# Two gated long convolutions: phases of two units on four row tiles, cosines in SBUF, one N=96 spectrum shape, and a new order

## The chip, the cores and the metric

The kernel runs on one core of one Trainium2 chip. The metric is the device time of one execution in microseconds. The engines are TensorE (PE, whose weight loads are listed apart as PEld), VectorE (DVE), ScalarE (ACT), GpSimd (POOL) and SyncE (SP, which here only issues DMAs). DVE, ACT and PE reach PSUM; POOL works on SBUF alone.

## The reference

Two diagonal state-space layers A and B read the same input `u` (2048 positions, 512 channels). Each has 128 complex modes a channel. A gate mixes the two outputs:

```python
A = -jnp.exp(log_A_real) + 1j * A_imag
C = (C_real + 1j * C_imag) * dt[:, None]
P = jnp.exp((A * dt[:, None])[:, :, None] * pos[None, None, :])
K = 2.0 * jnp.einsum("dn,dnl->dl", C, P).real          # a kernel of 2048 taps for each channel
y = jnp.fft.irfft(jnp.fft.rfft(K, L2) * jnp.fft.rfft(u_t, L2), L2)[:, :, :L]
...                                                    # y + u * D_skip is a (or b)
g = _sigmoid((x * gate_w).sum(-1, keepdims=True))
return g * a + (1 - g) * b
```

## The kernel before

**Units.** Layer and channel together give 1024 rows; 16 of them make a unit, so there are 64 units. For a unit the kernel writes the tap index as l = 64 m + q (32 values of m, 64 of q) and each mode's term as a product of one factor in m and one in q. Each factor is a decay times a cosine or sine:

- `phase` computes turns for the q half (`p0s`) and the m half (`p1s`) on PE, eight f16 matmuls in four accumulation steps: constants `cph` against `ones` or against `rot`, which holds the modes' turns. The q half uses rows 0 to 63 of the array, the m half rows 64 to 127, so the two are two row tiles. `rot` is read back from a bounce in DRAM by `turns`.
- `magnitude`, `cosine`, `sine` on ACT: |turns|, then two Sin. The copy for the cosine (`p0c`, `p1c`) lies in PSUM, as `p0s` and `p1s` do.
- `grid0` and `grid1` on POOL (L520) build the decay factors `f0` (16 x 64 for each partition) and `f1` (16 x 32) from the table `bas` of 28 shifts for each row, filled by `make_bases` on ACT (L488). The table's layout is row by shift, so each of ACT's writes of one shift has a step of 28 elements and POOL's reads of eight shifts are contiguous.
- `cos_minus`, `cos_plus`, `sin_minus`, `sin_plus`, `one_cos`, `one_sin` on DVE (L543 to L563) multiply decay by cosine or sine: one input in SBUF, one in PSUM. The cosine products are written to the free half of `f0` and `f1`, the sine products over the decay.
- `modes` on PE (L571) contracts over the modes into `pk`, one bank for each unit; `keep` (ACT, L578) copies it to `ks`, `skip` (DVE, L581) adds the skip term to tap 0.

**Blocks.** Four units are a block; there are 16. Transforms are matmuls in two steps: `first` (L593), `s2` (L630). `xall` holds the half-transformed data: kernels of an even block, 32 columns of products `t2`, kernels of an odd block, and inputs `u` of two blocks. For an even block `s2` multiplies 32 kernels (N=64, in two column tiles of 64 weights each), for an odd block 32 kernels and the inputs of the next two blocks (N=128, full weights). `products` (DVE, L641) multiplies the kernel spectrum in PSUM with the input spectrum `v`, once for the real part's rows and once turned. For that `keep_v` (ACT, L650) copies two blocks' input spectra out of PSUM, `turn_v` and `both_v` (SP DMAs) move halves between partitions, and `negate_v` (DVE, L661) writes the negated half from SBUF to SBUF. `add_products` (POOL DMAs with add) joins the two products, `inverse` (PE, L679) and `keep_z` (ACT, L685) go back, and `final` with its copies and DMAs turns four finished blocks at a time into output. `gate` (L760), once at the start, sums `u * gate_w` over channels for all positions, with the result on all 128 partitions.

**Order.** Every operation is recorded in a list and then built in the order of the table `ORDER` (2462 numbers); each engine executes its instructions in just that order. `SLOTS` names the PSUM bank of each PSUM tile. The grids' buffers `f0` and `f1` are two deep, so POOL's grid for a unit waits for `modes` of the unit two before.

```python
    for n in ORDER or range(len(ops)):
        key, name, fn, args = ops[n]
        fn(*args)
```

Of the kernel before, what the change touches and what calls it, by code (L numbers as in the profile page):

```python
# [11 lines left out]
F32 = mybir.dt.float32  # L12
# [174 lines left out]
]  # L187


SLOTS = [  # L190
    int(c) for c in (
        "012121212013230145460125463737251467615702561324560702376267021420713301314031031731206743"
# [804 lines left out]
```

## Time and profile before

| | |
|---|---|
| timed runs, us | 568.38, 570.80, 572.99 (median 570.8) |
| span of the profiled execution, us | 568.5 (nothing that lies around it is listed) |
| mean granted TensorE clock | 0.921 |
| PE, PEld, DVE, ACT, POOL busy, us | 458.2, 371.7, 412.8, 426.0, 342.6 |
| instructions | 26964 |
| costliest group on each engine | POOL L520 203.4 us, PE L630 109.4, DVE L641 91.4, ACT L488 50.6 |
| DMA | 49.84 MB, 88 GB/s on average |

A row of the view of groups reads: line, engine, operation, output <- inputs, shapes, count | busy us together, mean ns of one | idle time of the engine before them and what ended it. Busy time is the union of the instructions' spans: instructions of ACT and DVE overlap their neighbours by 0.05 to 0.2 us, and matmul rows include their latency, so that start to start times are shorter than the means. A matmul on f32 data shows as two rows of the trace. A row of the waits reads: engine and line that waited <- who ended the wait: us in total, times, longest.

### The profile page before, as it was taken

Reading aid. Unit: us, or ns where it says so; the run is one execution under the profiler, and the core shown is the slowest. Engines: PE = TensorE matmul, PEld = TensorE weight load, DVE = VectorE, ACT = ScalarE, POOL = GpSimd, SP = SyncE. Lnnn points to the kernel's source line nnn. Section 1 sums busy time; section 2 is a strip of 40 time slices with the busy share of each in tenths; the row PEclk is TensorE's granted clock in tenths of the full one; section 3 lists DMA queues with packets and bytes.
Section 4 is the critical chain, followed back from the end, with each engine's and each line's share of the span. In section 5 each row is a group of like instructions: output and inputs, shape, how many; then the busy total and the mean of one; then the engine's idle time right before and its main releaser. Section 6 shows DMA issues by size and latency. Waiting matters only on the chain.

```text
span 568.5 us, 26964 instructions
## 1 busy us (share of the span) xinstructions
PE 458.2 (81%) x11888; PEld 371.7 (65%) x11888; DVE 412.8 (73%) x826; ACT 426.0 (75%) x967; POOL 342.6 (60%) x324
## 2 busy tenths in 40 slices
PE   8557986879777898868997986968997979859756
PEld 8445456657575676767775774856785757748746
DVE  7096876888967983798689855698689896788210
ACT  4788879969986998867997994949987777565311
POOL 1549986989999877346766653435727664455120
PEclk9797989989988997998999996989997997989779
DMA  3649423460423515044506323044505250163242
GB/s 102 216 130 315 188 58 50 105 131 22 91 48 89 110 38 114 33 98 83 110 7 134 81 51 76 32 96 91 95 21 115 40 96 22 31 131 64 44 74 77
DMA packets 30772, 49.84 MB, mean 88 GB/s; under 512 B 10048, under 2 KB 15680, under 8 KB 30656
## 3 DMA queue, kind: packets, MB, share of 16 engines
q1 hardware_dynamic: 25536, 31.34, 18.6%
q0 software_dynamic: 5120, 16.78, 17.8%
q8 instruction: 93, 1.52, 1.1%
q14 instruction: 23, 0.19, 0.1%
HBM read 17.18 MB, written 5.77 MB: 40 GB/s over the span
## 4 chain that ended last, share of the span: by engine, by line
PE 29%; ACT 17%; DVE 15%; issue 7%; POOL 5%; DMA 1%; ACTq 0%; DVEq 0%; POOLq 0%
PE pk L571 6%; PE psi L679 6%; DVE xall L641 5%; PE p0s L504 5%; DVE v L661 4%; ACT bas L488 4%; PE ps L630 4%; PE ps L593 3%; PE pf L699 3%; ACT xall L600 2%; PE pl L733 1%; ACT p1c L510 1%; ACT z L685 1%; ACT p0c L516 1%; ACT p0c L510 1%
## 5 line engine op out<-in xcount | busy, mean ns | idle before, releaser
L520 POOL TENSOR_TENSOR f<-bas 128x512 f32<-128x512 f32 (+1 forms) x128 | 203.4, 1670 | 119.1 <-PE pk L571 49.3
L630 PE MATMUL ps<-xall,gk 128*64 128x64 f32 (+1 forms) x1728 | 109.4, 252 | 13.3 <-ACT v L650 4.3
L630 PEld LDWEIGHTS ps<-xall,gk 128*64 128x64 f32 (+1 forms) x1728 | 102.4, 155 | 24.8 <-issue 6.6
L641 DVE TENSOR_TENSOR xall<-ps,v 128x256 f32<-128x256 f32 x256 | 91.4, 418 | 26.1 <-PE ps L630 21.1
L571 PE MATMUL pk<-f,f 128*32 128x64 f32 x4096 | 79.1, 231 | 23.7 <-DVE f L551 13.2
L571 PEld LDWEIGHTS pk<-f,f 128*32 128x32 f32 x4096 | 67.3, 117 | 35.0 <-issue 24.4
L669 POOL DMA_DIRECT2D xall<-xall x64 | 60.0, 1203 | 48.0 <-ACT z L685 22.6
L679 PE MATMUL psi<-mi,xall 128*128 128x128 f32 x512 | 74.8, 303 | 11.4 <-DMA xall<-xall 6.8
L679 PEld LDWEIGHTS psi<-mi,xall 128*128 128x128 f32 x512 | 67.8, 211 | 22.5 <-issue 10.7
L559 DVE TENSOR_TENSOR f<-f,p1c 128x512 f32<-128x512 f32 x64 | 43.7, 684 | 25.8 <-ACT p1c L516 23.8
L543 DVE TENSOR_TENSOR f<-f,p0c 128x512 f32<-128x512 f32 x64 | 43.6, 683 | 24.5 <-ACT p0c L516 22.6
L504 PE MATMUL p0s<-cph,ones 64*128 64x512 f16 x128 | 52.8, 412 | 9.2 <-ACT xall L600 3.9
L593 PE MATMUL ps<-w,ks 64*64 64x64 f32 x2048 | 41.9, 231 | 16.2 <-issue 8.1
L685 ACT COPY z<-psi 128x512 f32<-128x512 f32 x64 | 38.5, 620 | 21.5 <-PE psi L679 21.5
L504 PE MATMUL p1s<-cph,ones 64*128 64x512 f16 x128 | 53.0, 414 | 0.7 <-DVE f L559 0.7
L593 PEld LDWEIGHTS ps<-w,ks 64*64 64x64 f32 x2048 | 36.6, 144 | 25.3 <-issue 11.8
L504 PE MATMUL p0s<-cph,rot 64*128 64x512 f16 x128 | 52.4, 409 | 0.2 <-issue 0.2
L504 PE MATMUL p1s<-cph,rot 64*128 64x512 f16 x128 | 52.4, 409 | 0.0
L488 ACT ACTIVATE bas<-dec 128x128 f32<-128x128 f32 x192 | 50.6, 490 | 0.8 <-DVE dec L423 0.7
L510 ACT ACTIVATE p1c<-p1s 128x512 f32<-128x512 f32 x64 | 38.2, 597 | 16.9 <-PE p1s L504 8.1
L510 ACT ACTIVATE p0c<-p0s 128x512 f32<-128x512 f32 x64 | 38.8, 607 | 15.4 <-PE p1s L504 5.7
L563 DVE TENSOR_TENSOR f<-f,p1s 128x512 f32<-128x512 f32 x64 | 43.7, 684 | 5.7 <-ACT p1s L513 4.3
(130 smaller groups left out, 866.7 us busy)
## 6 DMA issues: line engine op xcount, KB each, us to landing
xall<-xall POOLq DMA_DIRECT2D x64, 256.0 KB, 5.3
v<-v SPq DMA_DIRECT2D x64, 128.0 KB, 3.3
uraw<-in_us SPq DMA_DIRECT2D x16, 256.0 KB, 4.2
z<-in_ut SPq DMA_DIRECT2D x16, 256.0 KB, 6.8
out_dram<-ot SPq DMA_DIRECT2D x24, 128.0 KB, 2.4
par<-in_par SPq DMA_DIRECT2D x8, 256.0 KB, 5.2
gk<-in_gk SPq DMA_DIRECT2D x4, 512.0 KB, 7.0
eg<-in_eg SPq DMA_DIRECT2D x4, 512.0 KB, 7.2
```

What stands on the lines that cost most here:

```text
L488: S.activation(bas[:, c % 2, :, j], decays[c][:, 0], AF.Exp, scale=-float(s))
L504: PE.matmul(ps, w[h : h + 64], cph[h : h + 64, j], start=j == 0, stop=j == 3, tile_position=(h, 0))
L510: S.activation(pc[u], ps[u], AF.Abs)
L520: G.tensor_tensor(o.rearrange("p k (a b) -> p k a b", b=8), x[:, :, hi : hi + n].unsqueeze(3).to_broadcast([128, 16, n, 8]), x[:, :, lo : ...
L559: V.tensor_tensor(f[:, 0], f[:, 1], p1c[u], OP.mult)
L571: PE.matmul(pk[32 * kd : 32 * kd + 32, i, :], f1[:, p, 4 * i + kd, :], f0[:, p, 4 * i + kd, :], start=p == 1, stop=p == 0, tile_position=( ...
L593: PE.matmul(ps[h][64 * ri : 64 * ri + 64, n, :], x[r], w1[r, ri, r], start=True, stop=True, tile_position=(64 * h, 64 * ri),)
L630: PE.matmul(ps[h : h + w, j, 0:n], gk[:, k, h : h + w], xall[:, x0:x1, 2 * k : 2 * k + 2], start=True, stop=True, tile_position=(0, h),)
L641: V.tensor_tensor(k.rearrange("p x (k t) -> p k x t", t=2), p2s[b, g][:, :, 0:64].rearrange("p k (x t) -> p k x t", t=2), vv.unsqueeze(3). ...
L669: G.dma_start(out=xk(b)[o, s], in_=t2[t, s], accum_op=OP.add)
L679: PE.matmul(ps[:, i, :], xk(b)[:, x : x + 2, :].rearrange("p x k -> p (x k)"), mi, start=True, stop=True)
L685: S.copy(z[:, :, d0 : d0 + 4], pis[b, g].rearrange("p i r -> p r i"))
```

## The change

- **Phases.** `phase` handles two units at once on four row tiles of 32 rows: the q halves of both on tiles 0 and 1 (N=512), the m halves on tiles 2 and 3, whose steps with `rot` are two matmuls of N=256 each. `rot` is laid out for that and loaded by six DMAs a chunk of eight units instead of two.
- **Cosines in SBUF.** `p0c` and `p1c` become SBUF tiles (four buffers), so the three cosine products read two SBUF inputs. The sine products come first and go to the free half; the cosine products go over the decay. `pk` and `ks` hold two units, so `keep` and `skip` run 32 times, not 64.
- **Spectra.** `xall` holds 32 kernels, the inputs of one odd block, of one even block, 32 kernels, then `t2`. Blocks 0 to 14 all use N=96 with full weights; the last block N=64; the input of block 0 alone N=32. `keep_v` runs for every block (128 copies of 128 elements instead of 64 of 256).
- **Second products.** `negate_v` goes. A DMA `same_v` copies the half, and the product takes the sign from `halfs`, +1 or -1 for each partition: two scalar-tensor-tensors with a step of 2 instead of one tensor-tensor. `v` is now turned for each block: 96 DMAs instead of 64.
- **Decay table.** `bas` is shift by row: ACT writes contiguously, POOL reads the shifts with a step of 128 elements.
- **Gate.** `gate_parts` sums four channel groups into 32 partitions each (four column tiles), `gate_keep` copies to SBUF, and a matmul with 1/32 everywhere sums them.
- **Order.** `ORDER` and `SLOTS` are new.

```diff
-    11, 2, 0, 6, 1, 3, 4, 5, 74, 15, 19, 20, 21, 23, 22, 25, 24, 29, 40, 26, 27, 45, 12, 28, 18,
+    11, 0, 1, 19, 20, 21, 22, 23, 24, 5, 74, 25, 26, 28, 27, 30, 31, 32, 75, 33, 29, 34, 4, 2, 35, 36, 40, 37, 45,
...
-    t2 = xall[:, 32:64]
+    t2 = xall[:, 96:128]
-    rot = const.tile([128, 2, 8, 128], F16, name="rot")
-    bas = const.tile([128, 2, 128, 28], F32, name="bas")
+    rot = const.tile([128, 2, 4, 2, 128], F16, name="rot")
+    bas = const.tile([128, 2, 28, 128], F32, name="bas")
...
-    def phase(u):
-        p0s[u], p1s[u] = bank("p0s"), bank("p1s")
+    def phase(q):
+        us = (2 * q, 2 * q + 1)
+        ps = [bank(n) for n in ("p0s", "p0s", "p1s", "p1s")]
+        for n, u in enumerate(us):
+            p0s[u], p1s[u] = ps[n], ps[2 + n]
+        w = rot[:, q // 4 % 2, q % 4]
         for j in range(4):
-            for h, ps in ((0, p0s[u]), (64, p1s[u])):
-                w = rot[:, u // 8 % 2, u % 8] if j % 2 else ones
-                PE.matmul(
-                    ps, w[h : h + 64], cph[h : h + 64, j], start=j == 0, stop=j == 3, tile_position=(h, 0)
-                )
+            for h in range(2):
+                for t in range(4):
+                    rows = slice(32 * t, 32 * t + 32)
+                    halves = j % 2 and t > 1
+                    if h and not halves:
+                        continue
+                    cols = slice(256 * h, 256 * h + 256) if halves else slice(0, 512)
+                    PE.matmul(
+                        ps[t][:, cols], w[rows, h] if j % 2 else ones[rows], cph[rows, j, cols],
+                        start=j == 0, stop=j == 3 and h == (t > 1), tile_position=(32 * t, 0),
+                    )
 
     def magnitude(u, ps, pc, name):
-        pc[u] = bank(name)
+        pc[u] = work.tile([128, 512], F32, name=name, tag="pc", bufs=4)
...
     def grid(u, o, hi, n, lo):
-        x = bas[:, u // 8 % 2, 16 * (u % 8) : 16 * (u % 8) + 16, :]
+        x = bas[:, u // 8 % 2, :, 16 * (u % 8) : 16 * (u % 8) + 16].rearrange("p s k -> p k s")
...
     def s2(b, g):
-        x0, x1 = 64 * (b % 2), 64 * (b % 2) + 32
+        x0, x1 = 48 * (b % 2), 48 * (b % 2) + 48
         if b < 0:
-            x0 = x1
-        if b % 2 and b < nblk - 1:
-            x1 += 32
+            x1 = x0 + 16
+        elif b == nblk - 1:
+            x0 += 16
...
     def products(b, g, second):
...
+        if second:
+            for t in range(2):
+                V.scalar_tensor_tensor(o[:, :, :, t], k[:, :, :, t], halfs, vv, op0=OP.mult, op1=OP.mult)
+        else:
+            V.tensor_tensor(o, k, vv.unsqueeze(3).to_broadcast([128, 4, 32, 2]), OP.mult)
...
-    def negate_v(i, h):
-        V.tensor_scalar(v_at(hi, i, 1, h), v_at(hi, i, 0, h), -1.0, None, op0=OP.mult)
+    def same_v(b, h):
+        dma(v_at(hi, b, 1, h), v_at(hi, b, 0, h))
...
+    def gate_parts(j):
+        psg[j] = bank("psg")
+        for sb in range(nsb):
+            PE.matmul(
+                psg[j][32 * sb : 32 * sb + 32], gw[:, sb : sb + 1].to_broadcast([128, 32]), ut(sb, j),
+                start=True, stop=True, tile_position=(0, 32 * sb),
+            )
```

**On PE, a unit's phases.** The first steps of the first unit stood so before (`p0s_357` and `p1s_358` are its two banks):

```order
L504 LDWEIGHTS ones_73
L504 MATMUL p0s_357<-cph_72,ones_73 128x512
L504 LDWEIGHTS ones_73
L504 MATMUL p1s_358<-cph_72,ones_73 128x512
L504 LDWEIGHTS rot_83
L504 MATMUL p0s_357<-cph_72,rot_83 128x512
L504 LDWEIGHTS rot_83
L504 MATMUL p1s_358<-cph_72,rot_83 128x512
```

The step with `rot` of the first pair now, with one bank for each row tile (`p0s_402` and `p1s_404` belong to the pair's first unit):

```order
L493 LDWEIGHTS rot_84
L493 MATMUL p0s_402<-cph_72,rot_84 128x512
L493 LDWEIGHTS rot_84
L493 MATMUL p0s_403<-cph_72,rot_84 128x512
L493 LDWEIGHTS rot_84
L493 MATMUL p1s_404<-cph_72,rot_84 128x256
L493 LDWEIGHTS rot_84
L493 MATMUL p1s_405<-cph_72,rot_84 128x256
L493 LDWEIGHTS rot_84
L493 MATMUL p1s_404<-cph_72,rot_84 128x256
L493 LDWEIGHTS rot_84
L493 MATMUL p1s_405<-cph_72,rot_84 128x256
```

Four banks are filled in the steps that filled two, and a step with `rot` has six matmuls for two units where it had four.

**On DVE, around the products of a block.** Before, near the end of an odd block, the negations of the next input spectra (L661) stand between products (L641) and the cosine and sine products of later units:

```order
L641 TENSOR_TENSOR xall_78<-ps2_2645,v_77 128x4x32x2 x2
L547 TENSOR_TENSOR f0_2545<-f0_2545,p0c_2557 128x16x32
L551 TENSOR_TENSOR f0_2545<-f0_2545,p0s_2492 128x16x32
L555 SCALAR_TENSOR_TENSOR f0_2545<-f0_2545,p0s_2492 128x16x32
L581 TENSOR_TENSOR ks_2705<-pk_2655,dl_75 128x4
L661 TENSOR_SCALAR v_77<-v_77 64x512
L641 TENSOR_TENSOR xall_78<-ps2_2711,v_77 128x4x32x2 x2
L559 TENSOR_TENSOR f1_2707<-f1_2707,p1c_2717 128x512
L661 TENSOR_SCALAR v_77<-v_77 64x512
```

Now, in a block's products (L644 the first, L642 the second of a group):

```order
L547 TENSOR_TENSOR f0_2401<-f0_2401,p0c_2431 128x16x32
L644 TENSOR_TENSOR xall_79<-ps2_2489,v_78 128x4x32x2
L543 TENSOR_TENSOR f0_2401<-f0_2401,p0c_2431 128x16x32
L644 TENSOR_TENSOR xall_79<-ps2_2506,v_78 128x4x32x2
L551 TENSOR_TENSOR f1_2527<-f1_2527,p1s_2409 128x512
L555 TENSOR_TENSOR f1_2350<-f1_2350,p1c_2438 128x512
L642 SCALAR_TENSOR_TENSOR xall_79<-ps2_2506,small_69,v_78 128x4x32 x2
L642 SCALAR_TENSOR_TENSOR xall_79<-ps2_2476,small_69,v_78 128x4x32 x2
L642 SCALAR_TENSOR_TENSOR xall_79<-ps2_2496,small_69,v_78 128x4x32 x2
```

No negation is left, a second product is a pair of instructions, and among them stand cosine products (L543, L547, L555) whose two inputs, `f0` or `f1` and `p0c` or `p1c`, are both in SBUF.

More of the change, by code (lines that the diff above doesn't have):

```diff
@@ L278, in fixed @@
         V.memset(ones, ONE_W)
-        V.memset(rot[32:64], 0.0)
+        G.memset(thirty, 1.0 / 32)
         for b in range(2):
-            G.memset(bas[:, b, :, 0:24].rearrange("p c (s b) -> p c s b", b=8)[:, :, :, 0], 1.0)
+            G.memset(bas[:, b, 0:24].rearrange("p (s b) c -> p s b c", b=8)[:, :, 0], 1.0)
     def warm_up(n):
@@ L480, in turns @@
         i = next(i for i, cs in enumerate(BATCHES) if c in cs)
-        for h, t in zip((0, 64), dsps[i]):
-            src = t[BATCHES[i].index(c)].rearrange("(u k) d n -> (k d) u n", u=8)
-            dma(rot[h : h + 32 * (1 + h // 64), c % 2], src)
+        two, four = (t[BATCHES[i].index(c)] for t in dsps[i])
+        two = two.rearrange("(q u k) d n -> u (k d) q n", q=4, u=2)
+        four = four.rearrange("(q u s k) d n -> u s (k d) q n", q=4, u=2, s=2)
+        for u in range(2):
+            dma(rot[32 * u : 32 * u + 32, c % 2, :, 0], two[u])
+            for h in range(2):
+                dma(rot[64 + 32 * u : 96 + 32 * u, c % 2, :, h], four[u, h])
     def make_bases(c, n):
@@ L571, in modes, with keep, skip @@
                     PE.matmul(
-                        pk[32 * kd : 32 * kd + 32, i, :], f1[:, p, 4 * i + kd, :], f0[:, p, 4 * i + kd, :],
-                        start=p == 1, stop=p == 0, tile_position=(0, 32 * kd),
-                    )
-    def keep(u):
-        kss[u] = work.tile([128, 4, Q], F32, name="ks", tag="ks", bufs=4)
-        S.copy(kss[u], pks[u])
-    def skip(u):
-        V.tensor_tensor(kss[u][:, :, 0], pks[u][:, :, 0], dl[:, 4 * u : 4 * u + 4], OP.add)
+                        pks[q][32 * kd : 32 * kd + 32, 4 * h + i, :], f1[:, p, 4 * i + kd, :],
+                        f0[:, p, 4 * i + kd, :], start=p == 1, stop=p == 0, tile_position=(0, 32 * kd),
+                    )
+    def keep(q):
+        kss[q] = work.tile([128, 8, Q], F32, name="ks", tag="ks", bufs=2)
+        S.copy(kss[q], pks[q])
+    def skip(q):
+        V.tensor_tensor(kss[q][:, :, 0], pks[q][:, :, 0], dl[:, 8 * q : 8 * q + 8], OP.add)
     def xk(b):
@@ L602, in first_k @@
     def first_k(q):
-        first(q, "ps1", [kss[u][:, i, :] for u in (2 * q, 2 * q + 1) for i in range(4)])
+        first(q, "ps1", [kss[q][:, i, :] for i in range(8)])
     def keep_x(q, h):
@@ L760, in gate, with gate_keep @@
             PE.matmul(
-                psg[j], gw[:, sb : sb + 1].to_broadcast([128, 128]), ut(sb, j), start=sb == 0, stop=sb == nsb - 1
-            )
+                psg[j][32 * sb : 32 * sb + 32], gw[:, sb : sb + 1].to_broadcast([128, 32]), ut(sb, j),
+                start=True, stop=True, tile_position=(0, 32 * sb),
+            )
+    def gate_keep(j):
+        S.copy(ut(0, j), psg[j])
+    def gate(j):
+        psg[j] = bank("psg")
+        PE.matmul(psg[j], thirty, ut(0, j), start=True, stop=True)
     def gate_sig(j):
@@ L793, in unit @@
     def unit(u):
+        if u % 2 == 0:
+            op("ph", phase, u // 2)
         for name, fn in (
-            ("ph", phase), ("g0", grid0), ("g1", grid1),
-            ("a0", lambda u: magnitude(u, p0s, p0c, "p0c")), ("c0", lambda u: cosine(u, p0c)),
-            ("s0", lambda u: sine(u, p0s)), ("a1", lambda u: magnitude(u, p1s, p1c, "p1c")),
-            ("c1", lambda u: cosine(u, p1c)), ("s1", lambda u: sine(u, p1s)),
-            ("cm", cos_minus), ("cp", cos_plus), ("sm", sin_minus), ("sp", sin_plus), ("oc", one_cos),
-            ("os", one_sin), ("mo", modes), ("ke", keep), ("kd", skip),
+            ("g0", grid0), ("g1", grid1),
+            ("a0", lambda u: magnitude(u, p0s, p0c, "p0c")), ("s0", lambda u: sine(u, p0s)),
+            ("a1", lambda u: magnitude(u, p1s, p1c, "p1c")), ("s1", lambda u: sine(u, p1s)),
+            ("c0", lambda u: cosine(u, p0c)), ("c1", lambda u: cosine(u, p1c)),
+            ("sm", sin_minus), ("sp", sin_plus), ("os", one_sin), ("cm", cos_minus), ("cp", cos_plus),
+            ("oc", one_cos), ("mo", modes),
         ):
@@ L803, in unit @@
         if u % 2:
-            op("f1", first_k, u // 2)
+            q = u // 2
+            op("ke", keep, q)
+            op("kd", skip, q)
+            op("f1", first_k, q)
             for h in range(2):
-                op("xk", keep_x, u // 2, h)
+                op("xk", keep_x, q, h)
     def inputs(b):
@@ L814, in block @@
     def block(b):
-        nxt = b % 2 and b < nblk - 1
         for g in range(8):
@@ L826, in block @@
                     op("ya", add_products, b, h, x)
-        if nxt:
+        if b < nblk - 1:
             for h in range(2):
-                for i in range(2):
-                    op("vt", turn_v, i, h)
-                    op("vn", negate_v, i, h)
-                    op("vb", both_v, i, h)
+                op("vt", turn_v, b + 1, h)
+                op("vs", same_v, b + 1, h)
+                op("vb", both_v, b + 1, h)
     def back(b):
@@ L842, in tile_gated_s4d @@
     inputs(0)
-    inputs(1)
     chunk(0)
@@ L864, in tile_gated_s4d @@
         b, n = divmod(u, 4)
-        if b % 2 and n < 2 and b < nblk - 1:
-            inputs(b + 1 + n)
+        if n == 1 and b < nblk - 1:
+            inputs(b + 1)
         if n == 3:
@@ L887, in tile_gated_s4d @@
     last = {}
-    for n in ORDER or range(len(ops)):
+    for n in ORDER:
         key, name, fn, args = ops[n]
@@ L948, in _layout, with spread @@
     eg = np.tile(np.repeat(eg, 2, 0), (2, 1, 1, 1))
-    e16 = np.eye(16)
-    x = np.kron(e16, np.arange(32) + 0.5)
-    w = np.kron(e16, m - 16.0)
-    o = np.kron(e16, np.ones(32))
-    cph = np.zeros((2, 64, 4, 512))
-    cph[0, :32, 1] = np.stack([x, x / LOW], 1).reshape(32, 512)
-    cph[1, :, 1] = np.stack([w, w / LOW, o, o / LOW], 1).reshape(64, 512)
+    def spread(rows, d):
+        return np.einsum("ef,dj->edfj", np.eye(rows), np.stack(d)).reshape(rows * len(d), -1)
+    cph = np.zeros((4, 32, 4, 512))
+    x, w, o = np.arange(32) + 0.5, m - 16.0, np.ones(32)
+    cph[0:2, :, 1] = spread(16, [x, x / LOW])
+    cph[2:4, :, 1] = np.tile(spread(8, [w, w / LOW, o, o / LOW]), 2)
     cph[:, 0, 0], cph[:, 0, 2] = ONE_M, -ONE_M
@@ L958, in _layout @@
     cph = cph.reshape(128, 4, 512)
-    kern = np.arange(128) % 2
-    small = np.concatenate([ldt, 1 - 2 * kern[:, None], gw], 1)
+    kern = np.arange(128)[:, None] % 2
+    half = np.arange(128)[:, None] // 64
+    small = np.concatenate([ldt, 1 - 2 * kern, 1 - 2 * half, gw], 1)
     arrs = dict(
```

111 lines of the change are left out of this document (53 added, 58 removed), and 288 rows, old and new, of tables (ORDER, SLOTS).

## The prediction

> **What bounds the kernel now.** I read the busy times of the page first, then the middle of the run by windows, then the waits.
>
> ```profile
> PE 458.2 (81%) x11888; PEld 371.7 (65%) x11888; DVE 412.8 (73%) x826; ACT 426.0 (75%) x967; POOL 342.6 (60%) x324
> ...
> 30.00:540.00 510.00, 420.13 (x11249) 336.01 (x11250) 396.95 (x765) 402.62 (x915) 329.36 (x306) 0.93 0.37 84
> ...
> 100.00:150.00 50.00, 40.94 (x993) 33.01 (x995) 43.90 (x87) 45.14 (x102) 46.09 (x48) 0.97 0.37 83
> 150.00:200.00 50.00, 39.32 (x924) 31.26 (x916) 39.95 (x76) 41.57 (x98) 45.55 (x47) 0.93 0.41 84
> ```
>
> Columns of a window row: its length, then busy us of PE, weight loads, DVE, ACT and POOL (instructions in brackets), then the granted TensorE clock. Three engines are at 78 to 82% from 30 to 540 us, so no single one is the bound. The waits say the same:
>
> ```profile
> POOL f L520 <- PE pk L571: 49.3, 16, 6.0
> ...
> DVE f L559 <- ACT p1c L516: 23.8, 22, 3.0
> DVE f L543 <- ACT p0c L516: 22.6, 15, 12.3
> ...
> ACT z L685 <- PE psi L679: 21.5, 17, 8.3
> DVE xall L641 <- PE ps L630: 21.1, 15, 8.3
> ```
>
> POOL waits for PE (a grid buffer comes free when `modes` has read it), DVE for ACT's cosines and for PE, ACT for PE: a ring in which each hands on to the next.
>
> ```profile
> PE 29%; ACT 17%; DVE 15%; issue 7%; POOL 5%; DMA 1%; ACTq 0%; DVEq 0%; POOLq 0%
> ```
>
> The chain that ended last is spread over the same three. My estimate is therefore a sum over PE, DVE and ACT, and the middle 510 us is scaled by it; the first 30 and last 28.5 us I leave alone. The profiled execution's span is 568.5 us; what lies around it isn't listed, and the timed runs' median, 570.8, stands 2.3 us above it, which I add at the end.
>
> **The change part by part.**
>
> *Four row tiles* (L504 before). A unit's phases are four steps, two matmuls each:
>
> ```profile
> 300.14 0.39 PE L504 MATMUL p0s<-cph,ones 64*128 64x512 f16 x1
> 300.15 0.39 PE L504 MATMUL p1s<-cph,ones 64*128 64x512 f16 x1
> 300.37 0.38 PE L504 MATMUL p0s<-cph,rot 64*128 64x512 f16 x1
> 300.37 0.38 PE L504 MATMUL p1s<-cph,rot 64*128 64x512 f16 x1
> ...
> L504 PEld LDWEIGHTS <-ones 64*128 64x128 f16 x256 | 14.4, 98 | 25.3 <-issue 12.4 <-DVE f L547 1.2 <-DVE f L543 0.2
> ```
>
> The two of a step start 0.01 us apart, and steps start 0.22 us apart: the row tiles run together. A unit costs 4 x 0.22 = 0.88 us, 64 units 56 us. If four tiles run together as two do, a pair of units takes the same four steps (the second tile pair's 256-column halves follow each other inside a step), 32 x 0.88 = 28 us: **PE -28**. If they don't, 0; I take -28, the nearer row. A pair's 20 weight loads replace 16; I price them at nothing, since loads here run under the previous step's 0.22 us, and without that cover a load is 0.10 us. The Trainium skill's "TensorE: Matmul & The Clock Gate", Part 3, measured speedups, gives 3.07x, not 4x, for four row tiles at N=512; by that the step would stretch to 0.29 us and the gain would be about 19 us, an estimate. The trace of before shows two tiles at full overlap and never four.
>
> *N=96 spectra* (L630).
>
> ```profile
> L630 PE MATMUL ps<-xall,gk 128*128 128x128 f32 x448 | 55.3, 279 | 7.3 <-ACT v L650 4.3 <-ACT xall L600 2.9
> L630 PE MATMUL ps<-xall,gk 128*64 128x64 f32 x1280 | 54.1, 242 | 6.1 <-DVE xall L641 2.3 <-issue 1.4 <-DVE f L559 1.2
> L760 PE MATMUL psg<-z,small 128*128 128x512 f32 x32 | 14.8, 605 | 0.0
> ```
>
> A row costs 0.123 us at N=128 with all 128 columns of weights, and 0.042 us at N=64 with half of them. Fifteen blocks now have 64 rows each at N=96 and full weights, between 2 x 0.042 = 0.084 us and 0.123: 81 to 118 us. The last block keeps 128 x 0.042 = 5.4, the first has 128 rows at N=32, at most 5.4. Against 109.4 that is -18 to +20. Halfway by columns, 0.104, gives 100 + 11: **+1**.
>
> *Tiled gate* (L760): 32 rows at 0.46 us become four groups of 4 column tiles, two rows deep, and 8 rows of the summing matmul: 16 x 0.46 = 7.4. **PE -7**. If the column tiles ran one after the other it would be +4.
>
> *DVE.*
>
> ```profile
> L641 DVE TENSOR_TENSOR xall<-ps,v 128x256 f32<-128x256 f32 x256 | 91.4, 418 | 26.1 <-PE ps L630 21.1 <-issue 3.6 <-DMA rot<-dsp 0.4
> L661 DVE TENSOR_SCALAR v<-v 64x512 f32<-64x512 f32 x32 | 41.1, 1298 | 0.8
> L581 DVE TENSOR_TENSOR ks<-pk,dl 128x4 f32<-128x4 f32 x64 | 10.3, 161 | 35.3 <-ACT ks L578 34.9
> ...
> 12.05 0.28 DVE L383 TENSOR_TENSOR tb<-tb,sg 128x128 f32<-128x128 f32 x1
> 12.26 0.28 DVE L390 SCALAR_TENSOR_TENSOR rc<-rc,g 128x128 f32<-128x128 f32 x1
> ```
>
> The negations go: **-41**. Half of the 64 skip adds go: **-5**. Each of 128 second products (91.4/256 = 0.357 us) becomes two scalar-tensor-tensors of 128 elements. Such a one starts 0.21 us after its neighbour and lasts 0.28: 256 of them cost 54 to 72 instead of 46. I take the start to start, since they stand in pairs: **+8**. The cosines, read from SBUF, I price at 0.68 us as now, without a wait (the third rival is that wait).
>
> *ACT.*
>
> ```profile
> L488 ACT ACTIVATE bas<-dec 128x128 f32<-128x128 f32 x192 | 50.6, 490 | 0.8 <-DVE dec L423 0.7
> L685 ACT COPY z<-psi 128x512 f32<-128x512 f32 x64 | 38.5, 620 | 21.5 <-PE psi L679 21.5
> ...
> L578 ACT COPY ks<-pk 128x256 f32<-128x256 f32 x64 | 25.6, 402 | 28.2 <-PE pk L571 28.1
> L650 ACT COPY v<-ps 128x256 f32<-128x256 f32 x64 | 23.7, 397 | 12.1 <-DVE xall L641 8.7 <-PE ps L630 2.2 <-issue 0.6
> ...
> 265.27 0.35 ACT L357 ACTIVATE axy<-par 128x128 f32<-128x128 f32 x1
> 265.49 0.30 ACT L358 ACTIVATE pa<-par 128x128 f32<-128x128 f32 x1
> ```
>
> The 192 decay exponentials write every 28th element and take 50.6/192 = 0.264 us each; 128-element instructions with contiguous output stand 0.22 us apart. Turned, they save 0 to 8: **-8**. Kernel copies: 64 of 0.40 become 32 of 0.60, **-6**. Spectrum copies: 64 of 0.37 become 128 of 0.22 to 0.30, **+4 to +15**, I take **+8**. Gate copies: 4 x 0.60, **+2**. Abs into SBUF instead of PSUM: 0 (the SBUF copy's 0.60 is what Abs takes now).
>
> *Queues.*
>
> ```profile
> v<-v SPq DMA_DIRECT2D x64, 128.0 KB, 3.3
> ```
>
> SP issues 32 more copies of `v` and three times as many loads of `rot`. A block's chain from `keep_v` to products is paid every block instead of every second one, but it runs a block ahead, under four units' work; uncovered, it would be two landings in a row, 2 x 3.3 = 6.6 us a block.
>
> *Sum.* PE 458 - 28 + 1 - 7 = 424; DVE 413 - 41 - 5 + 8 = 375; ACT 426 - 8 - 6 + 8 + 2 = 422. Together 1221 against 1297, -5.9%. The middle becomes 510 x 0.941 = 480; with 58.5 around it 538.5, and **541 us** with the 2.3. ACT would stand at 78% of the span, below the 90% it holds from 100 to 150 us (45.14 of 50), so the sum asks nothing that this kernel doesn't reach already.
>
> **The rivals.**
>
> *Grids read at a stride.*
>
> ```profile
> L520 POOL TENSOR_TENSOR f<-bas 128x1024 f32<-128x1024 f32 x64 | 136.2, 2129 | 10.4 <-ACT bas L488 6.5 <-PE pk L571 3.9
> L520 POOL TENSOR_TENSOR f<-bas 128x512 f32<-128x512 f32 x64 | 76.9, 1211 | 108.7 <-PE pk L571 45.3 <-issue 23.4 <-DVE f L543 16.9
> ```
>
> The turned table makes POOL read its eight shifts 128 elements apart. No row shows POOL reading so. From 100 to 200 us POOL is 92% busy, 43 us of it grids (14 + 14 by the two rows' means: 28 of some 1.6 us), so there a grid that lasts half longer adds about 21 us to the path, and little elsewhere: 538 + 21 + 2 = **562 us**. The Trainium skill's "GPSIMD Engine Reference", Performance pitfalls for Q7 kernels, says that reads with a step above 8 bytes cost half more per element; no run here shows it yet.
>
> *DVE and POOL shut each other out.* Why the negations are so dear:
>
> ```profile
> 249.41 0.42 DVE L661 TENSOR_SCALAR v<-v 64x512 f32<-64x512 f32 x1
> ...
> 250.66 4.79 DVE L661 TENSOR_SCALAR v<-v 64x512 f32<-64x512 f32 x2
> ...
> 250.66 1.36 POOL L520 TENSOR_TENSOR f<-bas 128x512 f32<-128x512 f32 x1
> ...
> 252.26 2.55 POOL L520 TENSOR_TENSOR f<-bas 128x1024 f32<-128x1024 f32 x1
> ```
>
> Alone such an instruction takes 0.42 us; with grids running two took 4.79, and the mean is 1.30: 0.88 us of waiting each. It works from SBUF to SBUF. After the change 192 products (two `cos`, one `one_cos` a unit) have both inputs in SBUF. If each waits as the negation did, DVE gets 192 x 0.88 = 169 us more: 375 + 169 = 544. DVE's best window is 88% (43.90 of 50), so the span would be 544 / 0.88 = 618. At half that wait, 460 us busy, DVE needs 522 and decides nothing; it is slower than before from about 125 us of waits, 0.65 us each. Some waits would overlap idle time, so I price this case at **600 us**. Against it: a negation writes as well as reads at double rate, the products do not, and they need not meet POOL in the same way. The Trainium skill's "SBUF — State Buffer", Who interferes with whom, names just these, a DVE instruction with two SBUF inputs against a GpSimd instruction that reads SBUF, as exclusive; the trace agrees for the negation (0.42 to 4.79 us for two) and has no such product beside a grid.
>
> *The tiles don't run together, or the ring turns no faster.* Without the 28 us of PE, and with each wait that goes replaced by the next in the ring, 566 to 576: **570**.
>
> **How the numbers follow.** A measurement of this kernel can tell about 1% from no change: 565 to 576.5 is the same. The forecast, 525 to 555, gets 0.53; faster still, where the engines overlap better than now (ACT 422 at 82% of 515), 0.10; the strided grids 0.13, two thirds of it still faster; the unchanged ring 0.06; DVE and POOL shut out 0.18. Faster is 0.53 + 0.10 + 0.09 = 0.72, same 0.04 + 0.06 = 0.10, slower 0.18. By the open prices alone the sum's low end is 1221 - 19 (N=96) - 4 (spectrum copies) = 1198, 532 us; its high end 1221 + 28 (row tiles) + 19 (N=96) + 11 (gate) + 18 (second products) + 8 (decay) + 7 (spectrum copies) = 1312, 577 us. The range is 515 to 595: it takes these in, and leaves out a tenth above and less below.
>
> **What would show it.** Right: phase steps of four matmuls 0.22 us apart; N=96 rows about 0.10 us; DVE busy near 375 us with `cos` products at 0.68; ACT's decay at 0.22; spectrum products no longer waiting for copies of `v`. Wrong: products of `cos` at 1 us and more with the spread of the negations, grids at 2.9 and 1.6 us, DVE above 460 us busy, or POOL above 400.

## The result: 647.4 us against 570.5, and the profile after

The changed kernel takes 647.4 us (median of four runs, 644.9 to 649.5), the kernel before 570.5 in the runs beside it: a ratio of 1.135, 95% interval 1.129 to 1.140. The forecast was 541 us. The profiled execution's span is 646.2 us at a granted clock of 0.865 (before 568.5 at 0.921). Here and below a time is the median of all runs of a kernel, while a ratio and its 95% interval leave out runs that stand apart from the others, slow ones mostly, so the two can differ a little.

The page's busy times of the changed kernel, then two windows from its middle (length, then busy us of PE, weight loads, DVE, ACT, POOL, then the granted clock):

```profile
PE 483.9 (75%) x11512; PEld 420.5 (65%) x11512; DVE 514.5 (80%) x889; ACT 424.9 (66%) x1003; POOL 452.3 (70%) x325
...
200.00:300.00 100.00, 77.24 (x2196) 65.70 (x2196) 85.09 (x131) 75.11 (x174) 83.88 (x60) 0.90 0.34 74
300.00:400.00 100.00, 76.90 (x1856) 68.52 (x1859) 86.13 (x147) 68.54 (x175) 72.58 (x56) 0.85 0.36 76
```

ACT is where the forecast had it (424.9 against 422). DVE, forecast at 375, has 514.5, and POOL 452 in place of 343. In the middle DVE is now the busiest engine, at 85 to 86%, while PE and ACT, 82% and 79% busy in the middle before, have fallen back to 77% and 69 to 75%. The groups of DVE and POOL (count, then busy us and mean ns of one, then the idle time before them and what ended it) say what grew:

```profile
L555 DVE TENSOR_TENSOR f<-f,p1c 128x512 f32<-128x512 f32 x64 | 92.1, 1443 | 5.0 <-ACT p1c L506 3.8
L642 DVE SCALAR_TENSOR_TENSOR xall<-ps,small,v 128x128 f32<-128x128 f32 x256 | 84.1, 425 | 41.5 <-ACT v L648 25.3 <-PE ps L624 13.1 <-DMA xall<-xall 2.5
L547 DVE TENSOR_TENSOR f<-f,p0c 128x512 f32<-128x512 f32 x64 | 80.5, 1260 | 1.3 <-ACT p0c L506 0.9
L543 DVE TENSOR_TENSOR f<-f,p0c 128x512 f32<-128x512 f32 x64 | 79.6, 1244 | 0.6
L644 DVE TENSOR_TENSOR xall<-ps,v 128x256 f32<-128x256 f32 x128 | 50.9, 414 | 16.3 <-PE ps L624 8.9 <-ACT v L648 6.2 <-ACT bas L722 1.0
L551 DVE TENSOR_TENSOR f<-f,p1s 128x512 f32<-128x512 f32 x64 | 43.4, 677 | 7.3 <-POOL f L510 5.5 <-ACT p1s L503 1.5
...
L510 POOL TENSOR_TENSOR f<-bas 128x1024 f32<-128x1024 f32 x64 | 188.7, 2952 | 41.7 <-PE pk L565 25.2 <-DVE f L547 5.4 <-DVE f L551 2.7
L510 POOL TENSOR_TENSOR f<-bas 128x512 f32<-128x512 f32 x64 | 111.6, 1746 | 47.2 <-PE pk L565 46.7 <-issue 0.3
```

A sine product (L551, its second input in PSUM) still takes 0.68 us. The three cosine products, of the same shape with both inputs in SBUF, take 1.24 to 1.44: (1443 + 1260 + 1244 - 3 x 680) ns x 64 = 122 us more than before. The grids take 2.95 and 1.75 us in place of 2.13 and 1.21. Two stretches of the timeline (start, us, engine) show the two engines together:

```profile
470.56 0.67 DVE L533 TENSOR_TENSOR f<-f,p0s 128x512 f32<-128x512 f32 x1
471.16 5.91 DVE L547 TENSOR_TENSOR f<-f,p0c 128x512 f32<-128x512 f32 x1
...
470.13 1.78 POOL L667 DMA_DIRECT2D xall<-xall  x1
470.71 3.97 POOL L510 TENSOR_TENSOR f<-bas 128x1024 f32<-128x1024 f32 x1
473.42 1.68 POOL L359 TENSOR_TENSOR rc<-rc,g 128x128 f32<-128x128 f32 x1
473.83 2.68 POOL L510 TENSOR_TENSOR f<-bas 128x512 f32<-128x512 f32 x1
```

The sine product of 470.56 takes 0.67 us. The cosine product behind it starts 0.45 us after a grid and ends at 477.07, 0.56 us after the second grid (476.51): it sat out both grids and the small product between them. The grids are stretched as well, but less than the 3.97 us of the first one suggests: that row begins while POOL's DMA issue of 470.13 still runs (to 471.91), which leaves 2.77 us, and a grid takes 2.73 at its fastest. Grids that don't overlap the instruction before them by more than 0.05 us take up to 3.34 us, 0.6 more than the fastest and about the length of one product.

The waits (total us, times, longest us) show what this does to the others:

```profile
POOL f L510 <- PE pk L565: 71.9, 26, 7.2
PE pk L565 <- DVE f L555: 39.9, 19, 5.5
PEld pk L565 <- POOL f L510: 31.2, 12, 5.5
DVE xall L642 <- ACT v L648: 25.3, 19, 3.2
```

`modes` on PE waits for the cosine product, and POOL for `modes`. In the profile before, the largest such row of PE behind a product was this:

```profile
PE pk L571 <- DVE f L551: 13.2, 6, 3.6
```

The chain that ended last answers little here. Followed back, it breaks off after a fifth of the span, so its shares speak of the end alone:

```profile
PE 7%; issue 3%; DMA 3%; DVE 2%; POOL 2%; ACT 1%; POOLq 0%; DVEq 0%; ACTq 0%
```

### The profile page after: what moved, and what is told of

It reads as the page before. It is cut to its first block, busy times and chain, and to the rows that moved or that the text cites. A ratio compares the mean times of both kernels' runs of the same rounds, so it can differ in the third digit from the quotient of the medians.

```text
span 646.2 us, 26289 instructions
## 1 busy us (share of the span) xinstructions
PE 483.9 (75%) x11512; PEld 420.5 (65%) x11512; DVE 514.5 (80%) x889; ACT 424.9 (66%) x1003; POOL 452.3 (70%) x325
## 5 line engine op out<-in xcount | busy, mean ns | idle before, releaser
L510 POOL TENSOR_TENSOR f<-bas 128x1024 f32<-128x1024 f32 (+1 forms) x128 | 295.0, 2349 | 88.9 <-PE pk L565 71.9
L624 PE MATMUL ps<-xall,gk 128*128 128x96 f32 (+2 forms) x1216 | 144.6, 287 | 20.0 <-DVE xall L644 8.0
L624 PEld LDWEIGHTS ps<-xall,gk 128*128 128x128 f32 (+1 forms) x1216 | 134.5, 201 | 30.4 <-DVE xall L644 6.3
L642 DVE SCALAR_TENSOR_TENSOR xall<-ps,small,v 128x128 f32<-128x128 f32 x256 | 84.1, 425 | 41.5 <-ACT v L648 25.3
L555 DVE TENSOR_TENSOR f<-f,p1c 128x512 f32<-128x512 f32 x64 | 92.1, 1443 | 5.0 <-ACT p1c L506 3.8
L547 DVE TENSOR_TENSOR f<-f,p0c 128x512 f32<-128x512 f32 x64 | 80.5, 1260 | 1.3 <-ACT p0c L506 0.9
L543 DVE TENSOR_TENSOR f<-f,p0c 128x512 f32<-128x512 f32 x64 | 79.6, 1244 | 0.6
L644 DVE TENSOR_TENSOR xall<-ps,v 128x256 f32<-128x256 f32 x128 | 50.9, 414 | 16.3 <-PE ps L624 8.9
L537 DVE SCALAR_TENSOR_TENSOR f<-f,p0s 128x512 f32<-128x512 f32 x64 | 43.3, 677 | 11.8 <-ACT p0s L503 8.5
L533 DVE TENSOR_TENSOR f<-f,p0s 128x512 f32<-128x512 f32 x64 | 43.3, 677 | 9.6 <-POOL f L510 9.0
L594 ACT COPY xall<-ps 128x512 f32<-128x512 f32 x64 | 34.7, 590 | 24.6 <-PE ps L587 21.5
L551 DVE TENSOR_TENSOR f<-f,p1s 128x512 f32<-128x512 f32 x64 | 43.4, 677 | 7.3 <-POOL f L510 5.5
```

The source lines that it names most:

```text
L510: G.tensor_tensor(o.rearrange("p k (a b) -> p k a b", b=8), x[:, :, hi : hi + n].unsqueeze(3).to_broadcast([128, 16, n, 8]), x[:, :, lo : ...
L543: V.tensor_tensor(o, o, half(p0c[u], True), OP.mult)
L547: V.tensor_tensor(o, o, half(p0c[u], False), OP.mult)
L551: V.tensor_tensor(f[:, 1], f[:, 0], p1s[u], OP.mult)
L555: V.tensor_tensor(f[:, 0], f[:, 0], p1c[u], OP.mult)
L624: PE.matmul(ps[h : h + w, j, 0:n], gk[:, k, h : h + w], xall[:, x0:x1, 2 * k : 2 * k + 2], start=True, stop=True, tile_position=(0, h),)
```

## The experiments

Two theories. **Port:** the cosine products, which now read two SBUF inputs, and POOL's reads shut each other out (the port is the name of the theory; no profile shows one). **Stride:** POOL's grids, which now read `bas` 128 elements apart, are longer, and POOL's ring with `modes` sets the time. A third: the other edits (spectra, second products, order) cost what the phases save, or more. Line numbers differ by a few between the kernels below.

**One part alone on the kernel before.** First the cosines in SBUF, with nothing else changed:

```diff
-        pc[u] = bank(name)
+        next(slots)
+        pc[u] = work.tile([128, 512], F32, name=name, tag="pc", bufs=4)
```

> The kernel before with one thing changed: |turns| and cosine go to SBUF tiles instead of PSUM banks, so that three of the six DVE products a unit have two SBUF inputs. Port theory (DVE and POOL shut each other out): these 192 products rise from 0.68 us to a mean of 1.2 to 1.5 us, DVE busy from 413 to 510-560 us, and the time to 600-640 us. Stride theory (only the turned table costs) and order theory (the new order and the copies of v for every block cost): products stay at 0.68 us, the time stays at 565-576 us.

Measured: 611.7 us, ratio 1.069 (1.064 to 1.074). Its products on DVE:

```profile
L548 DVE TENSOR_TENSOR f<-f,p0c 128x512 f32<-128x512 f32 x64 | 67.6, 1056 | 2.0 <-ACT p0c L517 1.9
L544 DVE TENSOR_TENSOR f<-f,p0c 128x512 f32<-128x512 f32 x64 | 64.9, 1015 | 19.3 <-ACT p0c L517 17.2 <-POOL f L521 2.0
L560 DVE TENSOR_TENSOR f<-f,p1c 128x512 f32<-128x512 f32 x64 | 64.7, 1010 | 19.9 <-ACT p1c L517 19.2 <-POOL f L521 0.4
L564 DVE TENSOR_TENSOR f<-f,p1s 128x512 f32<-128x512 f32 x64 | 43.5, 681 | 2.7 <-ACT p1s L514 0.7
```

From 0.68 to 1.01 to 1.06 us by this edit alone, 67 us of DVE, and 39 us of time. Then the turned table alone:

```diff
-    bas = const.tile([128, 2, 128, 28], F32, name="bas")
+    bas = const.tile([128, 2, 28, 128], F32, name="bas")
...
-        x = bas[:, u // 8 % 2, 16 * (u % 8) : 16 * (u % 8) + 16, :]
+        x = bas[:, u // 8 % 2, :, 16 * (u % 8) : 16 * (u % 8) + 16].rearrange("p s k -> p k s")
```

> The kernel before with only the decay table turned (shift by row). Stride theory: undisturbed grids go from 1.95 and 1.07 us to 2.74 and 1.46, POOL busy from 343 to about 420 us, ACT falls by 8 to 10 us; if the stride by itself made the change slower, the time goes to 600 us or more. Port theory: grids longer, but nothing of the cosine products to collide with, so 570-590 us. Order theory: 565-576 us.

Measured: 616.4 us, 1.076 (1.071 to 1.081). Its grids and its window from 100 to 200 us:

```profile
L520 POOL TENSOR_TENSOR f<-bas 128x1024 f32<-128x1024 f32 x64 | 189.4, 2965 | 8.4 <-ACT bas L488 5.7 <-issue 2.7
L520 POOL TENSOR_TENSOR f<-bas 128x512 f32<-128x512 f32 x64 | 105.3, 1656 | 91.1 <-PE pk L571 43.5 <-issue 18.1 <-DVE f L543 16.4
...
100.00:200.00 100.00, 76.05 (x1540) 63.49 (x1539) 71.36 (x136) 75.73 (x187) 94.80 (x85) 0.86 0.35 73
```

Undisturbed (the fastest tenth) a strided grid takes 2.73 and 1.46 us where it took 1.94 and 1.06: +41% and +37%. So each edit costs some 7% alone. The second is not the stride's alone, though: the longer grids also hold up the negations, which this kernel still has, 1.76 us each in place of 1.30:

```profile
L661 DVE TENSOR_SCALAR v<-v 64x512 f32<-64x512 f32 x32 | 55.9, 1759 | 0.8
```

Both edits together:

> The kernel before with the two single edits at once: cosines in SBUF and the turned table. If the two costs add as they stand alone (6.9% and 7.6%), the ratio is 1.14 to 1.16 (650 to 660 us); if longer grids lengthen the products' waits as well (they can wait for 2.7 us instead of 1.9), 1.16 to 1.20; if one hides under the other, as two waits of one ring would, 1.08 to 1.11.

Measured: 685.8 us, 1.205 (1.199 to 1.210); alone they would multiply to 1.150. Longer grids make longer waits of the cosine products, 1.24 to 1.55 us, and the negations stand at 1.44 (1.30 before):

```profile
L560 DVE TENSOR_TENSOR f<-f,p1c 128x512 f32<-128x512 f32 x64 | 99.2, 1549 | 21.2 <-ACT p1c L517 18.4 <-POOL f L521 2.6
L544 DVE TENSOR_TENSOR f<-f,p0c 128x512 f32<-128x512 f32 x64 | 80.5, 1259 | 23.2 <-ACT p0c L517 14.3 <-POOL f L521 7.8 <-POOL tb L383 0.9
L662 DVE TENSOR_SCALAR v<-v 64x512 f32<-64x512 f32 x32 | 45.6, 1437 | 0.8
```

**Each cause taken out of the changed kernel.** The table by row and shift again, all else as changed (the reverse of the diff above):

> The changed kernel with the decay table laid row by shift again. Stride theory: grids back at 1.95 and 1.07 us undisturbed, POOL from 452 to about 370, ACT up by 10 us, and the time falls by 50 us or more, below 600. Port theory: the grids' lock on DVE gets shorter by the same third, so the cosine products fall from 1.3 to about 1.1 us on average, and the time by 15 to 35 us, to 612-632 us. Order theory: 640-650 us.

Measured: 606.9 us, 1.066 (1.059 to 1.072), below what the port theory expected and above what the stride theory did: both have a part. Cosine products 1.03 to 1.14 us. To take the port out, POOL has to stop reading while it stays as busy. Memsets of the undisturbed strided grids' length (1.80 + 0.95 and 0.94 + 0.52 us at their fastest) do that; the decay factors are left out:

```diff
-        grid(u, f0s[u][:, 0], 8, 8, 0)
+        G.memset(f0s[u].rearrange("p v k m -> p (v k m)"), 1.0)
+        G.memset(f0s[u][:, 0].rearrange("p k m -> p (k m)"), 1.0)
```

> The changed kernel with each grid on POOL replaced by two memsets of constant 1.0 into the same buffer, 3072 elements for the 16 x 64 grid (about 2.7 us) and 1536 for the 16 x 32 one (about 1.45 us): POOL is as long busy as the undisturbed strided grids, but reads nothing. The decay factors are left out of the result. Theory (DVE's second SBUF input and POOL's reads exclude each other): the cosine products come back to 0.68 to 0.75 us, DVE busy falls from 514 to about 400 us, and the time from 647 to 600 or less. Rival (DVE is slow for the SBUF operand itself, or for any traffic of POOL): the products stay above 1.2 us, DVE above 500 us, the time above 635 us.

Measured: 575.6 us, 1.008 (1.003 to 1.012), from busy times and groups:

```profile
PE 457.5 (80%) x11512; PEld 395.3 (69%) x11512; DVE 402.7 (70%) x889; ACT 421.9 (74%) x1003; POOL 424.1 (74%) x453
...
L557 DVE TENSOR_TENSOR f<-f,p1c 128x512 f32<-128x512 f32 x64 | 50.0, 785 | 3.8 <-ACT p1c L506 2.8
L549 DVE TENSOR_TENSOR f<-f,p0c 128x512 f32<-128x512 f32 x64 | 45.2, 707 | 0.5
L545 DVE TENSOR_TENSOR f<-f,p0c 128x512 f32<-128x512 f32 x64 | 44.0, 687 | 2.9 <-ACT p0c L506 2.6
```

The same products, both inputs still in SBUF, are back at 0.69 to 0.79 us, and 72 of the 77 us are back, with POOL 424 us busy. It is POOL's reading, not its being busy and not DVE's SBUF operand: of the 192 products the 18 that took over 0.75 us all ran beside an instruction of POOL that reads (a tensor-tensor, a copy, a tensor-scalar), none beside memsets alone. PE's busy time falls from 483.9 to 457.5 with its instructions unchanged, about in the ratio of the granted clocks (0.865 to 0.92): PE's growth goes with the clock. In most of these profiles the clock was lower where PE was busy for a smaller share (0.921 at 81% before, 0.892 at 78% with cosines alone, 0.847 at 72% with both edits); what sets it is not shown. Then memsets as short as the grids of before on average, 2.11 and 1.25 us (undisturbed, those grids take 1.94 and 1.06):

> As the kernel with memsets in the grids' place, but with memsets as long as the grids of before: 2304 elements (about 2.1 us) and 1280 (about 1.25 us). The decay factors are left out of the result. Port and stride are then both taken out of the changed kernel. If these two are the whole of the loss and the rest of the change brings what the forecast summed, the time is 535 to 560 us; if the rest of the change (spectra of N=96, second products of two instructions, the order) costs as much as the phases save, it is 565 to 585 us.

Measured: 568.2 us, 0.984 (0.980 to 0.988). Only three of its ten runs stand behind the ratio, 558.2 to 562.3 us; the other seven took 567.1 to 572.4, and the median of all ten is 0.999 of the median of the kernel before. Whether it is faster stays unclear. The same memsets in the kernel before:

> The kernel before with the same short memsets in the grids' place: the fair partner of the changed kernel with them. The decay factors are left out of the result. POOL reads nothing, so the negations should fall from 1.30 us towards 0.42 (28 us of DVE) and the time by 0 to 3%: 553 to 571 us. If memsets disturb DVE as the grids do, the negations stay at 1.3 and the time at 570.

Measured: 566.7 us, 0.999 (0.995 to 1.003). The negations fell only to 0.95 us, neither to 0.42 nor staying at 1.30. They wait for memsets too: of the 20 that took over 0.55 us, 11 had nothing but memsets beside them, such as this one, which ends 0.27 us after the memset of 309.22:

```profile
309.77 1.53 DVE L663 TENSOR_SCALAR v<-v 64x512 f32<-64x512 f32 x1
...
309.22 1.81 POOL L534 MEMSET f<- 128x2048 f32 x1
311.09 0.47 POOL L535 MEMSET f<- 128x256 f32 x1
```

So the negation, with one input, and the cosine products, with two, are held up by different things. This makes a square for the changed kernel, in ratios to the kernel before:

| | no port conflict | port conflict |
|---|---|---|
| short grids | 0.984 (short memsets) | 1.066 (table turned back) |
| long grids | 1.008 (long memsets) | 1.135 (as changed) |

The stride costs 0.024 without the conflict (0.013 by the medians) and 0.069 with it; the conflict 0.082 at short grids and 0.127 at long ones. What is left, 0.984 against 0.999 for the kernel before with the same memsets, is what the rest of the change brings there: 1.5% at best, and nothing by the medians (568.2 against 566.7 us). With both conflicts in place it brings more, 1.135 against the 1.205 of the kernel before with both edits, a part of it the negations that are gone. The memsets also drop the grids' wait for the table; the profile of before puts that at 6.5 us of POOL's idle time, in a ring where POOL waits anyway.

**The other edits on the kernel before.** Signed second products (the negation goes, a DMA copies):

```diff
-        V.tensor_scalar(v_at(hi, i, 1, h), v_at(hi, i, 0, h), -1.0, None, op0=OP.mult)
+        dma(v_at(hi, i, 1, h), v_at(hi, i, 0, h))
...
+                V.scalar_tensor_tensor(o[:, :, :, t], s[:, :, :, t], halfs, vv, op0=OP.mult, op1=OP.mult)
```

> The kernel before with only the signed second products: the negation on DVE becomes a copy by DMA, and each second product two scalar-tensor-tensors. Port theory: 32 negations that waited for POOL are gone (-41 us of DVE), the pairs cost 84 us instead of 46 (as measured after the change), DVE 413 - 41 + 38 = 410; the grids get a little shorter; time 560-575 us. If the dear second products were the main loss, 585 us or more.

Measured: 565.6 us, 0.979 (0.969 to 0.989), by two of four runs (0.988 by the medians), so unclear as a gain; DVE 401.4 us busy, 11 less than before. The signed products were not a main loss. Full weights for all spectra (`w = 128`):

> The kernel before with full 128-column weights in every spectrum matmul (even blocks N=64 in one tile instead of two column tiles). If the shape of the spectra is a main loss: PE's spectrum matmuls rise from 109 us by 20 us or more (rows of the even blocks at 0.12 us, 64 a block, instead of 128 at 0.042) and the time goes to 585 us or more. Port theory: PE rises by up to 20 us, but the time stays within 565-580 us.

Measured: 592.0 us, 1.022 (1.012 to 1.033), by two of four runs (1.034 by the medians): a loss, of unclear size. Its spectra by shape:

```profile
L630 PE MATMUL ps<-xall,gk 128*128 128x64 f32 x640 | 85.4, 294 | 4.5 <-ACT ks L578 1.4 <-DVE f L559 1.2 <-DVE xall L641 0.6
...
L630 PE MATMUL ps<-xall,gk 128*128 128x128 f32 x448 | 54.1, 276 | 7.7 <-ACT v L650 4.9 <-ACT xall L600 2.8
```

**A way out that was none.** The cosine products read the sine's bank `p0s` or `p1s` in PSUM (the cosine is left out of them), and 60 of the 192 products move forward in the order, so that the bank is free in time:

```diff
-        V.tensor_tensor(o, o, half(p0c[u], True), OP.mult)
+        V.tensor_tensor(o, o, half(p0s[u], True), OP.mult)
```

> The changed kernel, with the cosine products multiplying by the sine in PSUM instead of the cosine in SBUF (the cosine is computed and left out of the result; 60 of 192 products stand earlier in the order, since the sine's bank is given on). No DVE product of a unit has two SBUF inputs then. Port theory: these products fall from 1.25-1.44 to 0.68 us, DVE busy from 514 to about 395, and the time falls by 50 us or more, to 575-600 us. Stride theory: the time falls by less than 20 us (630 us or more). Order theory: 635-650 us.

Measured: 653.7 us, 1.146 (1.139 to 1.153), not the 575 to 600 of the port theory, though every product took 0.68 us and DVE fell to 396 us. The same with the table turned back:

> The changed kernel with both: products from PSUM (the cosine is computed and left out of the result) and the table row by shift. Port and stride theories together: the loss is gone, and the saved PE work shows: 535-570 us. Order theory (the new order, copies of v for every block, N=96): stays above 600 us.

Measured: 637.9 us, 1.116 (1.110 to 1.122). And, with plain tensor-tensors for second products besides (the sign is left out):

> As the run with both, and the second products as one tensor-tensor without the sign (the sign is left out of the result). If the pair of scalar-tensor-tensors at 0.33 us each costs what DVE pays (84 against 46 us), DVE falls by 38 us and the time by 5 to 25 us against the run with both; if DVE is no longer the bound there, by less than 5 us.

Measured: 636.3 us, 1.111 (1.102 to 1.119); DVE lost another 25 us and the time nothing. For a while this spoke against the port. Taking port and grids out of that kernel as well decided it:

> The changed kernel with the cosine products reading the sine's PSUM bank (the cosine is left out of the products) and earlier in the order, as in the run before, and with the grids replaced by memsets of 3072 and 1536 elements as well (the decay factors are left out too). POOL reads nothing and no product has two SBUF inputs, so the port can cost nothing here. With memsets alone the time was 576 us. If the products in PSUM cost time by themselves, because the bank of the sine is held until the last product has read it and the spectrum's matmul waits for the bank, the time is 620 to 655 us, near the 654 with the real grids. If not, it is 565 to 585 us, and the run with the cosine products in PSUM was slow because of the strided grids.

Measured: 656.3 us, 1.151 (1.142 to 1.159), with these waits:

```profile
DVE xall L622 <- PE ps L604: 64.2, 46, 6.3
...
PEld ps L604 <- DVE f L535: 26.0, 13, 3.6
...
PE ps L604 <- DVE f L535: 23.7, 13, 3.4
```

Without any conflict it is as slow: the spectrum's matmul (L604) waits for the product (L535) that still reads its PSUM bank, and the products of spectra wait for that matmul (64.2 us, against 16.0 in the kernel with memsets alone). This kernel lost by its banks or its moved products what it gained at the port; these two weren't told apart.

**The conflict that the kernel before has.** Its 32 negations moved to ACT:

```diff
-        V.tensor_scalar(v_at(hi, i, 1, h), v_at(hi, i, 0, h), -1.0, None, op0=OP.mult)
+        S.activation(v_at(hi, i, 1, h), v_at(hi, i, 0, h), AF.Copy, scale=-1.0)
```

> The kernel before with its 32 negations on ACT in place of DVE (a copy with scale -1, 64 x 512, about 0.55 us each). DVE loses 41 us of busy time, most of it waiting for POOL's reads; ACT gains 16 to 20 us. If the port's waits cost 0.6 us of time for each us of waiting, as the cosines in SBUF did, the time falls by 1 to 3%: 554 to 565 us. If ACT is the tighter engine, it stays at 565 to 575 us.

Measured: 553.3 us, 0.968 (0.960 to 0.976; 0.973 by the medians): faster than both kernels, by one changed line.

```profile
PE 456.6 (82%) x11888; PEld 371.6 (67%) x11888; DVE 375.4 (68%) x794; ACT 443.6 (80%) x999; POOL 341.1 (61%) x324
```

DVE lost 37 us and ACT gained 18, on an engine that was already the fuller one.

## Why the prediction was wrong, step by step

- **The step that failed** is the one on the cosines: "read from SBUF, I price at 0.68 us as now, without a wait". They took 1.24 to 1.44 us, and the memsets show that this wait is most of the loss (575.6 against 647.4 us).
- **Its rival was sized about right on DVE (544 us busy; 514.5 came) and judged wrong.** It put the point where the wait decides at 125 us, 0.65 us a product, by DVE's busy time over 0.88. Measured were 122 us, 0.64 a product, and the time was 13.5% longer. By that formula 514.5 us of DVE would fit in 585, and the 463.8 of the kernel with the table turned back, where the grids are as short as before, in 527; that kernel took 606.9. A wait in a ring costs well before its engine is full: the 113 us that the memsets took off the three products (122 less 9) were worth 72 us, 0.64 us for each (POOL's busy time fell by 28 us with them); in the single edit 67 us cost 39. The stated range ended at 595, below the rival's own 600. The forecast gave this rival 0.18 because "a negation writes as well as reads at double rate" and the products do not; by the runs the two differ beside memsets (0.95 against 0.69 to 0.79 us), but beside grids both wait. The Trainium skill's "SBUF — State Buffer", Who interferes with whom, says that a DVE instruction with two SBUF inputs contends with a GpSimd instruction that reads SBUF, not with one that only writes it. The runs agree on both halves: 1.24 to 1.44 us beside grids, 0.69 to 0.79 beside memsets. The negation, which the prediction took for an instance of it, is none: it has one input and waits for memsets as well. It showed that DVE and POOL can shut each other out, not that the products would.
- **The strided grids** were named and undersized: 21 us, since POOL is full only from 100 to 200 us. The turned table alone cost 44 (1.076), the longer waits of the negations included; in the changed kernel it cost 0.069 of 570, or 39, and 0.013 to 0.024 where memsets leave no conflict: most of its price is the conflict that it lengthens. The rivals were given chances as if only one could happen; both did, and each made the other dearer. All four signs of being wrong that the prediction named were there: products of 1 us and more, longer grids, DVE above 460 us and POOL above 400.
- **Phases: right.** All matmuls of the phases, as one line of each kernel (before, then after; length, PE busy, weight loads):

```profile
0.00:568.00 568.00, 74.30 (x512) 22.58 (x512) 0.92 0.38 88
...
0.00:646.00 646.00, 40.06 (x640) 19.66 (x640) 0.86 0.36 84
```

```profile
315.31 0.39 PE L493 MATMUL p0s<-cph,ones 32*128 32x512 f16 x2
315.32 0.39 PE L493 MATMUL p1s<-cph,ones 32*128 32x512 f16 x2
315.54 0.38 PE L493 MATMUL p0s<-cph,rot 32*128 32x512 f16 x2
315.54 0.38 PE L493 MATMUL p1s<-cph,rot 32*128 32x256 f16 x4
315.75 0.38 PE L493 MATMUL p0s<-cph,ones 32*128 32x512 f16 x2
```

  That is -34 us of busy time, which includes the matmuls' latency. The forecast of -28 counted from start to start, and so counted it came true: the steps of four matmuls stand 0.22 us apart as those of two did. By the 3.07x of the Trainium skill's "TensorE: Matmul & The Clock Gate", Part 3, the step would have been 0.29 us, an estimate; here the four tiles ran fully together.
- **N=96: mis-sized**, +35 us for +1:

```profile
L624 PE MATMUL ps<-xall,gk 128*128 128x96 f32 x960 | 133.3, 293 | 18.8 <-DVE xall L644 8.0 <-ACT xall L594 3.1 <-DVE f L551 2.5
```

  0.139 us a row, above the range's upper end of 0.123. "Halfway by columns" was the wrong rule: with full weights a row costs 0.133 us at N=64 (85.4/640 above), 0.139 at N=96 and 0.121 at N=128. In these rows N hardly matters; what was lost is the pair of half-weight tiles, 2 x 0.042.
- **Second products: mis-sized.** The 256 scalar-tensor-tensors and 128 tensor-tensors take 84.1 + 50.9 = 135 us where 256 products took 91.4: +44 for +8. One of 128 elements costs 0.33 us, nearly a product of 256 (0.36); the neighbours at 0.21 read SBUF contiguously, these read PSUM with a step of 2 (which of the two makes them dear is not shown). In the kernel before they are just as dear, but the negations that go with them pay for it: its DVE lost 11 us with that edit.
- **Decay and copies: right** for ACT, whose sum was 422 and is 421.9 to 424.9; the decay's 192 writes cost 40.8 us, 10 less:

```profile
L468 ACT ACTIVATE bas<-dec 128x128 f32<-128x128 f32 x192 | 40.8, 306 | 0.9 <-POOL f L510 0.8
```

- **The sum as a method** came within 2% where port waits are out: with the busy times of the kernel with short memsets, 466.5 + 404.0 + 421.3 = 1292 against 1297, it gives 569 us (568.2 measured); with those of the kernel with long ones, 457.5 + 402.7 + 421.9 = 1282, it gives 565, a gain of 1% where 575.6 was a loss of 1%: POOL, 54 us busier there, is no term of it. It falls short where a port wait is among the terms: for the negations on ACT it gives -37 + 18 = -19 of 1297, 8 us, and 16 to 18 came (2.7% by the medians, 3.2% by the ratio).

From the forecast to the result: 541; 565 with the busy times as they are without the conflict, most of it the two mis-sized prices; 576 with long grids that read nothing; 647 with grids that read.

## What to carry to other kernels

Before an operand moves from PSUM to SBUF, look for what GpSimd reads at that time: here a two-input product on DVE then waited for whole GpSimd instructions, and each us of it cost some 0.6 us of time although no engine was full. When two rivals in a forecast can happen together and one lengthens the other, price them together. To take such a conflict out of a kernel and size it, put memsets of the same length in the reader's place; and look at small groups with an odd mean (32 negations at 1.30 us with a fastest of 0.42), since moving them gained 3% here and the whole change lost 13.

## What the runs showed of the hardware

- Waiting goes both ways, but not alike: a cosine product took up to 6.43 us where it takes 0.68 alone, and a grid of 2.73 us up to 3.34 with a product in its way. POOL's memsets left DVE's tensor-tensors alone (0.69 to 0.79 us on average, none over 0.75 with only memsets beside it), but not the negation (0.95 us on average, 0.42 alone).
- A tensor-tensor on POOL whose inputs are read at a step of 512 bytes took 37 to 41% longer than with contiguous shifts (2.73 against 1.94 us, 1.46 against 1.06).
- A matmul row of f32 with full weights cost 0.12 to 0.14 us at N=64, 96 and 128 alike; two half-weight tiles at N=64 cost 0.085 together.
